# Four transposes by DMA in place of three, half-width first products, and a reordered copy at two joins

## The chip, the cores and the metric

The kernel runs on one core of a Trainium2 chip. The metric is the device time of one execution in microseconds (us), as the core's own clock has it; less is better. A profile is one execution, taken by the hardware profiler (a further one of 721.83 us for the kernel before); its span is about 1.7 us shorter than the timed figure of the same execution.

## The reference

```python
def _A_ref(x, wqkv, wo):            # 32 heads of 32, window of 8 keys, dilation 2
    q, k, v = split(x @ wqkv)
    ...                             # softmax over keys pos, pos-2, ..., pos-14
    return o @ wo

def _B_ref(x, w1, w3, w2):          # F = 3584
    return (silu(x @ w1) * (x @ w3)) @ w2

xn = layernorm(x)                   # x: 2048 tokens x 1024
s  = _A_ref(xn, wqkv, wo)
g  = silu(_B_ref(xn, w1, w3, w2))
return x + s * g
```

(Shortened: the index arithmetic of the attention is left out.)

## The kernel before

The kernel multiplies 2x2 block matrices with seven products in place of eight. Tokens lie in four blocks of 512; a pair of blocks makes the 2x2 form, and the sums and differences that the scheme needs are made on VectorE (`xs` from tokens, `sq`, `sk`, `sv` from weights). One group of products is this function. `pa`, `pe` and `pb` are PSUM buffers (two banks each, four such buffers in all); `act_copy` runs on ScalarE; `snap` is a saved copy of the first product, where it was made earlier.

```python
def seven(key, A, B, e11, e12, e22, e21, snap=None):
    a11, a12, a22, s1, s2, s3, s4 = A
    b11, b21, b22, t1, t2, t3, t4 = B
    ...                                          # pa = a11*b11, unless snap has it
    pe = bank2(f"e{key}")
    for i in I:
        mm(pe[:, i], s1[i], t1, True)            # the "inner" product
    pb = bank2(f"b{key}")
    act_copy(pb[:], pa[:] if snap is None else snap)
    sp5 = k4(f"p{key}")
    act_copy(sp5[:], pe[:])
    if snap is None:
        ...                                      # pa += a12*b21
        e11(pa)
        flush()
    for i in I:
        mm(pb[:, i], s2[i], t2, False)
    su2 = k4(f"u{key}")
    act_copy(su2[:], pb[:])
    flush()
    ...                                          # pe += s4*b22, pb += s3*t3
    def tail():                                  # the held product
        for i in I:
            mm(pb[:, i], a22[i], t4, False)
        e21(pb)
    pend.append(tail)                            # run by the next flush()
```

The normalized second block has to be transposed, tile by tile of 128 tokens. Three tiles go through the DMA queue of SyncE, one through TensorE, and its result is copied out by ScalarE:

```python
def flip(st, eng):
    cols = slice(st * P, (st + 1) * P)
    dst = b12[:, :, cols], xT[:, 2, :, cols]
    if eng == "dma":
        for a in I:
            anchor["tr1"] = nc.sync.dma_start(out=dst[a], in_=xt[1][:, st, a * CH:(a + 1) * CH], transpose=True)
        return
    tp = bank2(f"tq{st}")
    for k in range(KT):
        ...                                      # matmul(tp[...], lhsT=tile, rhs=ident)
    for a in I:
        act(nc.scalar.copy, out=dst[a], in_=tp[:, a].rearrange("p (k t) -> p k t", k=KH))
```

And these are the places where groups join:

```python
for n, cols in enumerate((slice(0, 3 * P), slice(3 * P, CH))):   # xs: three tiles, then one
    ...
qkv_seven(0, 0, wq0, wq1, sq, None, snap[0:2])
...
def tr(c):
    for sts in ([0, 1], [2, 3]):
        with behind("ln"):                       # layer norm of a later block, as early as DVE can
            ln_dve(c, sts)
...
qkv_seven(1, 1, wk0, wk1, sk, step)
flush()                                          # join 1
...
qkv_seven(0, 1, wq0, wq1, sk, step)
flush()                                          # join 2, the MLP follows
```

Of the kernel before, what the change touches and what calls it, by code (L numbers as in the profile page):

```python
# [17 lines left out]
def kernel(  # L18
# [11 lines left out]
    nc = tc.nc  # L30
    P = 128
    S, D, F = 2048, 1024, 3584
    Dh, W, DIL = 32, 8, 2
    KT = D // P
    KH = KT // 2
    CH = 512
# [9 lines left out]
    I = range(2)  # L46
# [33 lines left out]
    ident = const.tile([P, P], BF16, name="ident")  # L80
    nc.gpsimd.memset(ident[:], 0.0)
    nc.gpsimd.affine_select(
        out=ident[:], in_=ident[:], compare_op=ALU.not_equal, fill=1.0,
# [5 lines left out]
        out=ones4[:], in_=ones4[:], compare_op=ALU.is_ge, fill=0.0,  # L89
# [3 lines left out]
        out=ones4[:], in_=ones4[:], compare_op=ALU.is_ge, fill=0.0,  # L93
# [5 lines left out]
        out=maskb[0:32], in_=maskb[0:32], compare_op=ALU.is_ge, fill=-1.0e9,  # L99
# [11 lines left out]
    pb = keep.tile([P, W, P], BF16, name="pb")  # L111
    xT = keep.tile([P, 3, KH, CH], BF16, name="xT")
# [19 lines left out]
    def bank2(name):  # L132
        return psum.tile([P, 2, CH], FP32, tag="mm", name=name)

    def k4(name, shape=(2, CH), dt=FP32):
        return kk.tile([P, *shape], dt, tag="k4", name=name)
# [10 lines left out]
    def mm(ps, lhs, rhs, first):  # L147
        n = len(lhs)
        for k in range(n):
            with behind("pe") if "open" in anchor else nullcontext():  # L150
                anchor["pe"] = nc.tensor.matmul(  # L151
                    ps, lhsT=lhs[k], rhs=rhs[k], start=(first and k == 0),
                    stop=(k == n - 1), skip_group_check=not first,
                )
# [3 lines left out]

    def act_copy(out_, in_):
        with hp():  # L160
            nc.scalar.copy(out=out_, in_=in_)  # L161

    pend = []

    def flush():
        while pend:
            pend.pop(0)()

    def seven(key, A, B, e11, e12, e22, e21, snap=None):
        a11, a12, a22, s1, s2, s3, s4 = A  # L170
        b11, b21, b22, t1, t2, t3, t4 = B
        if snap is None:
            pa = bank2(f"a{key}")
            for i in I:
                mm(pa[:, i], a11[i], b11, True)
        pe = bank2(f"e{key}")
        for i in I:
            mm(pe[:, i], s1[i], t1, True)
        pb = bank2(f"b{key}")
        act_copy(pb[:], pa[:] if snap is None else snap)  # L180
        sp5 = k4(f"p{key}")
        act_copy(sp5[:], pe[:])
        if snap is None:
            for i in I:
                mm(pa[:, i], a12[i], b21, False)
            e11(pa)
            flush()
        for i in I:
            mm(pb[:, i], s2[i], t2, False)
        su2 = k4(f"u{key}")  # L190
        act_copy(su2[:], pb[:])
        flush()
        for i in I:
            mm(pe[:, i], s4[i], b22, False)
        e12(pe, su2)
        run_hooks()
        for i in I:
            mm(pb[:, i], s3[i], t3, False)
        e22(pb, sp5)
        bg(pace["n"])  # L200

        def tail():
# [4 lines that stand above are left out]
        pend.append(tail)  # L207
# [10 lines left out]
    xt = {}  # L218
    anchor = {}
# [7 lines left out]
    def behind(key):  # L227
        return tc.issue_after(anchor[key].ins) if key in anchor else nullcontext()

    def act(f, **kw):  # L230
        with hp(), behind("a"):
            anchor["a"] = f(**kw)
# [99 lines left out]
    def qkv_A(w0, w1_, st, g):  # L332
        v0 = w0.rearrange("p k (c two j) -> p k two j c", two=2, j=4)
        v1 = w1_.rearrange("p k (c two j) -> p k two j c", two=2, j=4)
        v3 = w0.bitcast(FP16).rearrange("p k (c two j) -> p k two j c", two=2, j=4)
        sv = [s.rearrange("p k (c j) -> p k j c", j=4) for s in st or ()]
        pick = lambda v, h: [[v[:, k, h, 2 * g + i, :] for k in range(KH)] for i in I]
        sp = lambda q: [[sv[q][:, k, 2 * g + i, :] for k in range(KH)] for i in I]
        if st is None:
            return pick(v0, 0), pick(v1, 0)  # L340
        return pick(v0, 0), pick(v1, 0), pick(v1, 1), sp(0), sp(1), pick(v3, 1), sp(2)
# [17 lines left out]
    def qkv_copy(t, c, j0):  # L359
        def f(ps, *a):  # L360
            d, fin = qkv_dst(t, c, j0)
            with hp():
                if a:
                    anchor["u"] = anchor.get("v")
                    anchor["v"] = nc.vector.tensor_add(d, ps[:], a[0][:])
                else:
                    nc.scalar.copy(out=d, in_=ps[:])
                fin()
        return f

    def qkv_seven(t, b, w0, w1_, st, mid=None, snaps=None):
        c0, c1 = 2 * b, 2 * b + 1
        for g in range(2):
            cp = lambda c, j0: qkv_copy(t, c, j0)
            seven(f"q{t}{b}{g}", qkv_A(w0, w1_, st, g), Bq[b],
                  cp(c0, 2 * g), cp(c1, 2 * g), cp(c1, 4 + 2 * g), cp(c0, 4 + 2 * g),
                  None if snaps is None else snaps[g])
            if mid is not None:
                mid(g)
# [122 lines left out]
    def run_hooks():  # L502
        while hooks:
            hooks.pop(0)()
# [472 lines left out]
    wq0 = qkv_load(0, 0, slot(2, (4, D)), 4)  # L977
    wq1 = qkv_load(0, 1, slot(6, (4, D)), 4)
# [9 lines left out]
    snap = [oT[:, i // 2, 4 * (i % 2):4 * (i % 2) + 4].rearrange("p j n -> p (j n)").bitcast(FP32).rearrange("p (i n) -> p i n", i=2) for i in range(4)]  # L988
# [26 lines left out]
    def root(st):  # L1015
        act(nc.scalar.activation, out=rstd[:, st:st + 1], in_=mv[:, st, 1:2], func=ACTF.Sqrt, bias=eps_t[:], scale=1.0)

    def apply(st, c=0):
        r = rstd[:, st:st + 1]
        dve(nc.vector.reciprocal, out=r, in_=r)  # L1020
        dve(
            nc.vector.tensor_scalar, out=xt[c][:, st, :], in0=xt[c][:, st, :], scalar1=mv[:, st, 0:1], scalar2=r,
            op0=ALU.subtract, op1=ALU.mult,
        )
# [60 lines left out]
    sq = rows(20, 6, FP16).rearrange("p (q k n) -> p q k n", q=3, k=4)  # L1085
    sq = [sq[:, q] for q in range(3)]
# [18 lines left out]
    b12 = rows(12, 2).rearrange("p (k n) -> p k n", k=KH)  # L1105
# [18 lines left out]
        st_half(st, 1, 1)  # L1124
        st_end(st)

    def flip(st, eng):
        cols = slice(st * P, (st + 1) * P)
        dst = b12[:, :, cols], xT[:, 2, :, cols]
        if eng == "dma":  # L1130
            for a in I:
                anchor["tr1"] = nc.sync.dma_start(out=dst[a], in_=xt[1][:, st, a * CH:(a + 1) * CH], transpose=True)
            return
        tp = bank2(f"tq{st}")
        for k in range(KT):
            with behind("pe"):
                anchor["pe"] = nc.tensor.matmul(
                    tp[:, k // KH, (k % KH) * P:(k % KH + 1) * P], lhsT=xt[1][:, st, k * P:(k + 1) * P], rhs=ident[:],
                    start=(k % KH == 0), stop=(k % KH == KH - 1), skip_group_check=True,
                )  # L1140
        for a in I:
            act(nc.scalar.copy, out=dst[a], in_=tp[:, a].rearrange("p (k t) -> p k t", k=KH))

    pf[0, 0], pf[0, 1] = pf[0], pf[1]
    s_q[1]()
# [6 lines left out]
    mean_var(1)  # L1152
    root(1)
    apply(0, 1)
    flip(0, "dma")
    first(1, 1)
    mean_var(2)
    apply(1, 1)
    flip(1, "dma")
    root(2)  # L1160
    second(1, 0)
    store(1, 0)
    second(1, 1)
    mean_var(3)
    apply(2, 1)
    root(3)
    store(1, 1)
    s_q[3]()
    apply(3, 1)
    flip(3, "dma")  # L1170
    first(2, 0)
    flip(2, "pe")
    first(2, 1)
    for g in range(2):
        second(2, g)
# [4 lines left out]

    Bq = B0, B_of(xT1[0], xT1[1], xT1[3], xs1)
    s_k = qkv_sums(wk0, wk1, sk, parts=True)
    for n, cols in enumerate((slice(0, 3 * P), slice(3 * P, CH))):
        s_k[n]()
        dve(nc.vector.tensor_sub, xs[:, 0, :, cols], b12[:, :, cols], xT[:, 0, :, cols])
        dve(nc.vector.tensor_sub, xs[:, 1, :, cols], xT[:, 2, :, cols], xs[:, 0, :, cols])
# [3 lines left out]
    with behind("ln"):  # L1190
        s_k[2]()
        s_k[3]()
    qkv_seven(0, 0, wq0, wq1, sq, None, snap[0:2])
    with behind("tr1"):
        x_load(3)
    def tr(c):
        for sts in ([0, 1], [2, 3]):
            with behind("ln"):
                ln_dve(c, sts)
        ln_tr(c, rows(*((16, 4), (12, 4))[c - 2]).rearrange("p (k n) -> p k n", k=KT))  # L1200

# [20 lines left out]
    qkv_seven(2, 0, *wv, sv, step0, snap[4:6])  # L1222
    pace["n"] = PACE[1]
    qkv_seven(1, 1, wk0, wk1, sk, step)
    flush()
    with behind("v"):
        qkv_sums(wq0, wq1, sk, True)
    qkv_seven(2, 1, *wv, sv, step)
    qkv_seven(0, 1, wq0, wq1, sk, step)
    flush()  # L1230
    spill = [(x_dram[:, i], xT1[(0, 1, 3)[i]]) for i in range(3)] + [(xs_dram[:, i], xs1[:, i]) for i in range(4)]

    def mid(b):
        drain(2 * b + 1)
        wo_prepare(b)
# [41 lines left out]
```

## Time and profile before

| | before |
|---|---|
| time, three executions | 721.73 us (721.68 to 721.85) |
| span of the profile | 720.1 us |
| TensorE busy | 712.5 us, 99% |
| VectorE busy | 625.6 us, 87% |
| ScalarE busy | 314.1 us, 44% |
| waits of TensorE after 15 us | five steps, 1.11 us in all |

In timeline lines the columns are start, length, engine, line of the kernel, operation, output and inputs, shape and count; square brackets tell how long the engine had been idle and what released it. TensorE (PE) streams its matmuls, so a gap shows as a step between starts that is longer than the columns need (0.2158 us for 512), not as a hole between an end and a start. The prediction below shows the page, the waits and the timelines of the parts concerned.

### The profile page before, as it was taken

What the parts mean: (1) busy time and instruction counts of PE and PEld (TensorE: products, weight loads), DVE (VectorE), ACT (ScalarE), POOL (GpSimd) and SP (SyncE); (2) the same over time, 40 slices, a digit from 0 to 9 for tenths busy, and PEclk for the clock granted to TensorE, in tenths of its full rate; (3) what the DMA queues carried; (4) which work ended last, traced back from release to release, by engine and by line L of the source; (5) the groups of instructions that cost most, each with busy time, mean ns of one, the idle gap of its engine ahead of it and who ended that gap; (6) DMA issues with size and microseconds to landing.
All of it is one profiled execution on the core that took longest, in us unless ns stands there. A gap on an engine that the chain in (4) does not pass through costs nothing.

```text
span 720.1 us, 8820 instructions
## 1 busy us (share of the span) xinstructions
PE 712.5 (99%) x3367; PEld 346.2 (48%) x3367; DVE 625.6 (87%) x697; ACT 314.1 (44%) x329; POOL 95.7 (13%) x162
## 2 busy tenths in 40 slices
PE   8999999999999999999999999999999999999997
PEld 6655565654444444444444444444444444444443
DVE  7996879779879878978999999969859989998975
ACT  5745334356545456555545311024464563120234
POOL 1011100012300000233111000000435004000001
PEclk9999999999999999999999999999999999999999
DMA  9956257867754523457756647469799444463616
GB/s 333 267 146 176 82 185 228 274 228 242 240 174 160 178 85 117 153 205 264 251 169 216 203 132 240 155 189 385 172 279 348 127 152 138 156 205 130 194 55 117
DMA packets 119242, 139.52 MB, mean 194 GB/s; under 512 B 17696, under 2 KB 94496, under 8 KB 118560
## 3 DMA queue, kind: packets, MB, share of 16 engines
q1 hardware_dynamic: 104656, 97.01, 43.3%
q0 software_dynamic: 14544, 41.95, 17.9%
q8 instruction: 26, 0.43, 0.3%
q14 instruction: 16, 0.13, 0.1%
HBM read 96.21 MB, written 38.80 MB: 187 GB/s over the span
## 4 chain that ended last, share of the span: by engine, by line
PE 93%; DVE 2%; ACT 1%; DMA 1%; issue 1%; SPq 0%; DVEq 0%; ACTq 0%
PE bm L151 20%; PE am L151 13%; PE em L151 13%; PE bq L151 9%; PE db L151 8%; PE da L151 7%; PE de L151 6%; PE eq L151 6%; PE aq L151 3%; PE wb L151 3%; PE af L151 2%; PE wa L151 1%; PE we L151 1%; PE af L1038 1%; DMA wring<-in_A_wqkv_dram 1%
## 5 line engine op out<-in xcount | busy, mean ns | idle before, releaser
L151 PEld LDWEIGHTS <-wring 128*128 128x128 f16 (+1 forms) x1792 | 183.4, 103 | 204.2 <-issue 1.6
L151 PEld LDWEIGHTS <-h_sb 128*128 128x128 f16 (+1 forms) x1056 | 109.6, 104 | 118.1 <-issue 0.4
L151 PE MATMUL bm<-xs,wring 128*128 128x512 f16 x504 | 117.4, 379 | 0.1
L151 PE MATMUL am<-xT,wring 128*128 128x512 bf16 x336 | 79.7, 379 | 0.1
L151 PE MATMUL db<-wring,h_sb 128*128 128x512 f16 x336 | 73.2, 379 | 0.0
L481 DVE TENSOR_TENSOR BC<-Ep,vT 128x2048 bf16<-128x2048 bf16 x56 | 66.6, 1216 | 0.1
L426 DVE TENSOR_TENSOR pt<-qt,kT 128x4096 bf16<-128x4096 bf16 x24 | 54.9, 2289 | 0.6
L664 DVE TENSOR_TENSOR um<-em,um 128x1024 f32<-128x1024 f32 x28 | 34.2, 1222 | 21.1 <-PE em L151 20.3
L666 ACT ACTIVATE g<-um 128x1024 bf16<-128x1024 f32 x28 | 29.6, 1057 | 48.6 <-DVE um L664 48.6
L151 PE MATMUL da<-wring,h_sb 128*128 128x512 bf16 x224 | 49.0, 379 | 0.0
L467 POOL DMA_DIRECT2D Ep<-pb x64 | 38.0, 601 | 54.0 <-DVE pb L463 48.3
L151 PE MATMUL bm<-h_sb,wring 128*128 128x512 f16 x168 | 39.7, 379 | 0.0
L151 PE MATMUL em<-xT,wring 128*128 128x512 bf16 x168 | 39.7, 379 | 0.0
L151 PE MATMUL em<-xs,wring 128*128 128x512 f16 x168 | 39.7, 379 | 0.0
L161 ACT COPY bm<-am 128x1024 f32<-128x1024 f32 x28 | 27.9, 998 | 26.0 <-PE am L151 26.0
L491 DVE TENSOR_TENSOR oT<-oT,BC 128x2048 bf16<-128x2048 bf16 x32 | 39.0, 1218 | 0.3
L161 ACT COPY pm<-em 128x1024 f32<-128x1024 f32 x28 | 28.4, 1013 | 20.0 <-PE em L151 20.0
L161 ACT COPY um<-bm 128x1024 f32<-128x1024 f32 x28 | 28.4, 1013 | 18.9 <-PE bm L151 18.9
L685 ACT CAST g<-bm 128x1024 bf16<-128x1024 f32 x28 | 28.3, 1010 | 17.4 <-PE bm L151 17.4
L679 DVE TENSOR_TENSOR h_sb<-bm,pm 128x1024 bf16<-128x1024 f32 x21 | 25.6, 1217 | 5.1 <-PE bm L151 5.0
L428 DVE TENSOR_TENSOR pt<-pt 128x2048 bf16<-128x2048 bf16 x24 | 29.3, 1221 | 0.4
L489 DVE TENSOR_TENSOR BC<-BC 128x2048 bf16<-128x2048 bf16 x24 | 29.3, 1220 | 0.4
(191 smaller groups left out, 996.4 us busy)
## 6 DMA issues: line engine op xcount, KB each, us to landing
wring<-in_B_w_dram SPq DMA_DIRECT2D x61, 512.0 KB, 4.4
wring<-t_dram SPq DMA_DIRECT2D x16, 512.0 KB, 3.9
t_dram<-wring POOLq DMA_DIRECT2D x14, 512.0 KB, 3.9
wring<-t_dram SPq DMA_DIRECT2D x16, 384.0 KB, 5.0
wring<-in_B_w_dram SPq DMA_DIRECT2D x12, 384.0 KB, 4.8
wring<-in_A_x_dram SPq DMA_DIRECT2D x16, 256.0 KB, 4.7
Ep<-pb POOLq DMA_DIRECT2D x64, 64.0 KB, 4.7
wring<-in_A_wo_dram SPq DMA_DIRECT2D x8, 512.0 KB, 5.7
```

The costliest lines, as they stand in the source:

```text
L151: anchor["pe"] = nc.tensor.matmul(ps, lhsT=lhs[k], rhs=rhs[k], start=(first and k == 0), stop=(k == n - 1), skip_group_check=not first,)
L161: nc.scalar.copy(out=out_, in_=in_)
L426: nc.vector.tensor_mul(p_t[:], q[:], kT[:, :, o:o + CH])
L428: nc.vector.tensor_add(p_t[:, 0:4, :], p_t[:, 0:4, :], p_t[:, 4:8, :])
L467: nc.gpsimd.dma_start(out=pr[c][r:P:NR, :, sq * P:(sq + 1) * P], in_=pb[sq * 32:(sq + 1) * 32, :, :])
L481: nc.vector.tensor_mul(dst, E[:, w, :].unsqueeze(1).to_broadcast([P, n, CH]), vT[:, js, o:o + CH])
L489: nc.vector.tensor_add(B, B, C)
L491: nc.vector.tensor_add(A, A, B if w0 else C)
L664: v = nc.vector.tensor_add(su2[:], pe[:], su2[:])
L666: nc.scalar.activation(out=hl["g"][:, :, CH:], in_=su2[:], func=ACTF.Silu)
L679: anchor["v"] = nc.vector.tensor_add(h[:, :, CH:], pb[:], sp5[:])
L685: nc.scalar.copy(out=hl["g"][:, :, 0:CH], in_=pb[:])
```

## The change

The intent is to take work and gaps out of TensorE's stream. All four tiles of the second block are transposed by DMA. Since the last tile then lands later, the sums `xs` are made in two halves of two tiles, and the first q products run in token halves: first the half that is there. The inner product of the next group (`eq1`) follows at once, so that ScalarE has time to copy out the first. At the two joins the held product isn't forced to the front any more, and its copy is told to go behind the copy that TensorE waits for. The layer norm of later blocks goes behind the adds of the first group.

```diff
     def act_copy(out_, in_):
         with hp():
-            nc.scalar.copy(out=out_, in_=in_)
+            return nc.scalar.copy(out=out_, in_=in_)
 ...
-        pe = bank2(f"e{key}")
-        for i in I:
-            mm(pe[:, i], s1[i], t1, True)
+        pe = early.pop(key)() if key in early else bank2(f"e{key}")
         pb = bank2(f"b{key}")
-        act_copy(pb[:], pa[:] if snap is None else snap)
         sp5 = k4(f"p{key}")
-        act_copy(sp5[:], pe[:])
+        if key == "q000":
+            act_copy(pb[:], snap)
+            for th in I:
+                cols = slice(th * 2 * P, (th + 1) * 2 * P)
+                for ps, A1, B1 in ((pe, s1, t1), (pb, s2, t2)):
+                    ...                      # matmuls of 256 columns
+            act_copy(sp5[:], pe[:])
+            early["q001"]()
+        else:
+            ...
+            anchor["pb"] = act_copy(pb[:], pa[:] if snap is None else snap)
+            act_copy(sp5[:], pe[:])
 ...
                 else:
-                    nc.scalar.copy(out=d, in_=ps[:])
+                    with behind("pb"):
+                        nc.scalar.copy(out=d, in_=ps[:])
 ...
-    def flip(st, eng):
+    def flip(st):
+        for a, d in enumerate((b12[:, :, cols], xT[:, 2, :, cols])):
+            anchor["tr1"] = nc.sync.dma_start(out=d, in_=xt[1][:, st, a * CH:(a + 1) * CH], transpose=True)
 ...
-    for n, cols in enumerate((slice(0, 3 * P), slice(3 * P, CH))):
+    for n, cols in enumerate((slice(0, 2 * P), slice(2 * P, CH))):
 ...
-    qkv_seven(0, 0, wq0, wq1, sq, None, snap[0:2])
+    early["q001"] = eq1                      # q001's s1*t1, 16 matmuls as before
+    qkv_seven(0, 0, wq0, wq1, sq, lambda g: anchor.setdefault("q0", anchor["v"]), snap[0:2])
 ...
-            with behind("ln"):
+            with behind("q0"):
                 ln_dve(c, sts)
 ...
     qkv_seven(1, 1, wk0, wk1, sk, step)
-    flush()
 ...
     qkv_seven(0, 1, wq0, wq1, sk, step)
-    flush()
```

More of the change, by code (lines that the diff above doesn't have):

```diff
@@ L167, in flush @@
             pend.pop(0)()
+    early = {}
     def seven(key, A, B, e11, e12, e22, e21, snap=None):
@@ L175, in seven @@
                 mm(pa[:, i], a11[i], b11, True)
-        pe = bank2(f"e{key}")
-        for i in I:
-            mm(pe[:, i], s1[i], t1, True)
+        pe = early.pop(key)() if key in early else bank2(f"e{key}")
         pb = bank2(f"b{key}")
-        act_copy(pb[:], pa[:] if snap is None else snap)
         sp5 = k4(f"p{key}")
-        act_copy(sp5[:], pe[:])
+        if key == "q000":
[3 more added lines that the diff above has]
+                for ps, A1, B1 in ((pe, s1, t1), (pb, s2, t2)):
+                    for i in I:
+                        for k in range(KH):
+                            with behind("pe"):
+                                anchor["pe"] = nc.tensor.matmul(
+                                    ps[:, i, cols], lhsT=A1[i][k], rhs=B1[k][:, cols], stop=(k == KH - 1),
+                                    start=(ps is pe and k == 0 and th == 0), skip_group_check=True,
+                                )
+            act_copy(sp5[:], pe[:])
+            early["q001"]()
+        else:
+            if key != "q001":
+                for i in I:
+                    mm(pe[:, i], s1[i], t1, True)
+            anchor["pb"] = act_copy(pb[:], pa[:] if snap is None else snap)
+            act_copy(sp5[:], pe[:])
         if snap is None:
@@ L187, in seven @@
             flush()
-        for i in I:
-            mm(pb[:, i], s2[i], t2, False)
+        if key != "q000":
+            for i in I:
+                mm(pb[:, i], s2[i], t2, False)
         su2 = k4(f"u{key}")
@@ L1125, in mean_var @@
         st_end(st)
-    def flip(st, eng):
+    def flip(st):
         cols = slice(st * P, (st + 1) * P)
-        dst = b12[:, :, cols], xT[:, 2, :, cols]
-        if eng == "dma":
-            for a in I:
-                anchor["tr1"] = nc.sync.dma_start(out=dst[a], in_=xt[1][:, st, a * CH:(a + 1) * CH], transpose=True)
-            return
-        tp = bank2(f"tq{st}")
-        for k in range(KT):
-            with behind("pe"):
-                anchor["pe"] = nc.tensor.matmul(
-                    tp[:, k // KH, (k % KH) * P:(k % KH + 1) * P], lhsT=xt[1][:, st, k * P:(k + 1) * P], rhs=ident[:],
-                    start=(k % KH == 0), stop=(k % KH == KH - 1), skip_group_check=True,
-                )
-        for a in I:
-            act(nc.scalar.copy, out=dst[a], in_=tp[:, a].rearrange("p (k t) -> p k t", k=KH))
+        for a, d in enumerate((b12[:, :, cols], xT[:, 2, :, cols])):
+            anchor["tr1"] = nc.sync.dma_start(out=d, in_=xt[1][:, st, a * CH:(a + 1) * CH], transpose=True)
     pf[0, 0], pf[0, 1] = pf[0], pf[1]
@@ L1154 @@
     apply(0, 1)
-    flip(0, "dma")
+    flip(0)
     first(1, 1)
@@ L1158 @@
     apply(1, 1)
-    flip(1, "dma")
+    flip(1)
     root(2)
@@ L1165 @@
     apply(2, 1)
+    flip(2)
     root(3)
@@ L1169 @@
     apply(3, 1)
-    flip(3, "dma")
+    flip(3)
     first(2, 0)
-    flip(2, "pe")
     first(2, 1)
@@ L1192, with eq1 @@
         s_k[3]()
-    qkv_seven(0, 0, wq0, wq1, sq, None, snap[0:2])
+    def eq1():
+        pe = bank2("eq001")
+        for i in I:
+            for k in range(KH):
+                with behind("pe"):
+                    anchor["pe"] = nc.tensor.matmul(
+                        pe[:, i], lhsT=qkv_A(wq0, wq1, sq, 1)[3][i][k], rhs=Bq[0][3][k], start=(k == 0), stop=(k == KH - 1),
+                    )
+        early["q001"] = lambda: pe
+    early["q001"] = eq1
+    qkv_seven(0, 0, wq0, wq1, sq, lambda g: anchor.setdefault("q0", anchor["v"]), snap[0:2])
     with behind("tr1"):
```

## The prediction

> **What bounds the kernel now.** I read the page first: busy shares and the slices of the span.
>
> ```profile
> span 720.1 us, 8820 instructions
> PE 712.5 (99%) x3367; PEld 346.2 (48%) x3367; DVE 625.6 (87%) x697; ACT 314.1 (44%) x329; POOL 95.7 (13%) x162
> ...
> PE   8999999999999999999999999999999999999997
> ...
> PEclk9999999999999999999999999999999999999999
> ```
>
> TensorE (PE) is busy from the second slice to the last at full granted clock. A busy PE is not yet a gapless one, so next came the waits of PE alone:
>
> ```profile
> engine line waited for: us in total, times, longest us
> PE warm L142 <- DVE warm L139: 1.3, 1, 1.3
> PE tp L993 <- DVE wring L236: 1.0, 1, 1.0
> PE af L1038 <- ACT xT L1000: 0.5, 1, 0.5
> ```
>
> These are the only waits listed for PE, and all end before 9 us. Third, PE's timeline, which begins each group where the last one stops streaming: eight 128x512 matmuls start 1.73 us apart all through the kernel, 0.2158 us each. I took the step from each matmul's start to the next and subtracted the time its columns need. After 12 us only five steps stand out: 0.28 us at 110.7, 0.24 at 160.0, 0.28 at 286.9, 0.22 at 504.6 and 0.09 at 714.4; the five-row block sums (`zp`) aside, everything else is back to back. So the time is the sum of PE's instructions plus about 1.1 us. Whatever the change does counts only where it shortens that stream, closes one of those gaps or opens a new one.
>
> The parts concerned, from PE's timeline (start, length, operation, count):
>
> ```profile
> 24.13 1.89 PE L151 MATMUL af<-xT,wve 128*128 128x512 bf16 x8
> 25.86 0.61 PE L1137 MATMUL tq<-ident,wring 128*128 128x128 bf16 x8
> 26.30 5.35 PE L151 MATMUL af<-xT,wve 128*128 128x512 bf16 x24
> 31.49 1.89 PE L151 MATMUL eq<-xs,h_sb 128*128 128x512 f16 x8
> ...
> 107.25 1.89 PE L151 MATMUL bq<-h_sb 128*128 128x512 f16 x8
> 108.97 0.38 PE L151 MATMUL aq<-h_sb,wve 128*128 128x512 bf16 x1
> 109.19 1.89 PE L151 MATMUL eq<-h_sb,wring 128*128 128x512 f16 x8
> 111.20 1.89 PE L151 MATMUL aq<-h_sb,wve 128*128 128x512 bf16 x8
> ```
>
> Three things are to be seen. The transposes of one tile by matmul take the stream from 25.86 to 26.30. The q products (`eq`) follow at once at 31.49. And `aq` at 111.20 comes 2.01 us after `eq`, not 1.73: that is the join between two products. The chain of waits says why:
>
> ```profile
> 107.41 1.74 PE bq L151 x8
> 109.15 0.03 ACTq L367
> 109.18 0.04 issue
> 109.22 1.01 ACT pk L367
> 110.23 0.92 ACT bq L161
> 111.15 0.04 issue
> 111.20 1.89 PE aq L151 x8
> ```
>
> At the join the held product (`bq`, the tail of the group before) runs first; ScalarE (ACT) copies it out (`pk`) before it makes the copy of `aq` into `bq` that lets PE overwrite `aq`. PE waits for the second copy. The join at 160 is the same: `h_sb<-bq` at 158.50, `bm<-am` from 159.41 to 160.43, PE at 160.48.
>
> **What the Trainium skill says.** "TensorE: Matmul & The Clock Gate", Back-to-back issue gap, gives N/2.4 + 2.5 ns for warm matmuls: 55.8, 109.2 and 215.8 ns for 128, 256 and 512 columns. The trace agrees: 0.44/8 = 55 ns for `tq`, 4.37/40 = 109 ns for the 128x256 products at 12.85 to 17.22, 1.73/8 = 216 ns. (The 131 ns sustained of the same section is not what this kernel shows.) "VectorE: DVE Perf Modes", The three transpose paths, gives a DMA transpose of 128x128 as 1309 ns; here one issue, of four such blocks, holds the queue for 1.19 to 1.32 us, so the figure fits an issue, not a block. "DMA: Bandwidth & Descriptors", Rules for kernel authors, advises to issue a DMA early and wait late; whether this one is early enough is the question below.
>
> **The change part by part.** The built order of instructions of the changed kernel differs only before about 162 us; from there on PE, ACT and DVE hold the same order.
>
> 1. The fourth tile of the second block is transposed by DMA too. PE loses 8 matmuls: -0.44 us. ACT loses two copies (0.58 and 0.60 us), which are off the path. The DMA queue gains two issues. This is the queue's timeline before:
>
> ```profile
> 23.58 1.21 SPq L1132 DMA_TRANSPOSE h_sb<-wring  x1
> 24.84 1.26 SPq L1132 DMA_TRANSPOSE xT<-wring  x1
> 26.70 1.19 SPq L1132 DMA_TRANSPOSE h_sb<-wring  x1
> 27.93 1.27 SPq L1132 DMA_TRANSPOSE xT<-wring  x1
> ```
>
> Tile 2 is normalized by 24.9, so its issues follow at 26.15 and 27.40, and tile 3's at about 28.7 and 29.95, ending near 31.2 instead of 29.20. The last two of before landed 1.1 us after their issues ended (29.03 and 30.31). So tile 3 lands at about 31.1 and 32.35, 2 us later than before.
>
> 2. The sums `xs` on VectorE (DVE) are split 2+2 tiles instead of 3+1, and the first q products run in token halves: `eq` half, `bq` half, `eq` half, `bq` half, then the next group's inner product. From these DVE lines
>
> ```profile
> 27.90 0.96 DVE L236 TENSOR_TENSOR xs<-h_sb,xT 128x1536 f16<-128x1536 bf16 x1
> ...
> 29.82 1.22 DVE L236 TENSOR_TENSOR h_sb<-h_sb,wring 128x2048 f16<-128x2048 f16 x1
> 30.95 0.42 DVE L236 TENSOR_TENSOR xs<-h_sb,xT 128x512 f16<-128x512 bf16 x1
> ```
>
> a 1024-wide sum is about 0.69 us. First halves: 27.9 to 28.6 and 28.7 to 29.4; `h_sb` to 30.5; then DVE waits for the landing at 31.1: second halves 31.2 to 31.9, and 32.45 to 33.15. PE reaches the q products at 31.49 - 0.45 = 31.04 and needs the four quarters at 31.04, 31.91, 32.77 and 33.64 (0.864 us each). Margins: 2.4, 2.5, 0.9 and 0.5 us. So no wait, but the last is thin. The halves cost 32 x 109.2 - 16 x 215.8 ns = +0.04 us. The next group's inner product (1.73 us) gives ACT time: `eq` is complete at 33.6, copied by 34.8, and overwritten from 36.2; `bq` at 34.5, copied by 36.8, overwritten from 37.95.
>
> 3. The layer norm of blocks 3 and 4 on DVE is put behind the first group's adds. I walked DVE's new order with the old durations: it ends near 66.9 instead of 65.7, with the last normalized tile at 63.4 instead of 56.8. Its transposes land before 70. Their sums start at 74.3, and PE reads the result at 81 to 83. No cost.
>
> 4. At the two joins the held product no longer comes first. `aq` or `am` is complete 1.73 us earlier against the copy that PE waits for, and ACT is told to make that copy first: -0.28 and -0.24 us. At the second join the order is `am` x8, held product x3, `em` x8, `am` x8, held product x5. `em` needs a weight sum of DVE, before at 156.73 to 157.41 while `em` started at 158.51. Now the sum ends at 157.41 - 0.73 = 156.68 and `em` could start at 156.70. With the weight load (103 ns) and the semaphore I allow +0.13 us.
>
> Sum: -0.44 - 0.28 - 0.24 + 0.04 + 0.13 = -0.79 us. 721.73 - 0.79 = 720.9 us.
>
> **The rivals.** (a) The DMA transposes land late, and PE waits where it had the matmul transposes. For: the queue is 2 us later, and the first two issues of before took 5.8 and 5.0 us to land, behind weight loads that ended at 26.1. Against: after 26.1 nothing else is in the queue, and the two last took 2.3 and 2.4. Each tenth beyond 0.5 us of delay is a tenth lost; 1 us more would leave 721.4. (b) The gaps at the joins only move: at the second join `em` waits for DVE, or the held product's late copy holds a PSUM buffer. For: DVE runs without idle from 155 to past 170. Against: `em` has needed this sum all along and misses it by little. If the whole of 0.24 comes back as this wait: 721.0; with a second one behind it: 721.3. (c) DVE, 87% busy, turns the delayed layer norm into waits: one of a few us would give 723 to 725. Against: it idles 5.7 us before 71.5. (d) All margins hold and `em` does not wait: 720.75.
>
> **Range and chances.** The change can take away at most about 1 us of PE's stream, and I see no stall over 1 us that it could open. I put 720.3 to 721.8 for 8 in 10: the low end is everything closed plus spread (runs of before lie 0.17 us apart), the high end a gain eaten whole by (a) or (b). Two per cent is 14 us: faster by that is impossible by the sum (0.5%), slower would need rival (c) several times over (1%), within 2% 98.5%.
>
> **What would show it.** PE's page row with 3375 matmuls (8 fewer, 16 more). `eq` near 31.05, four groups of eight 128x256 spaced 0.87, and no wait of PE there (wrong: a wait on DVE `xs` or a longer step). Transposes 7 and 8 landing near 31.1 and 32.4. `aq` at the first join 1.73 after `eq`. A step of 0.1 to 0.2 too long before `em` near 156.7. From 170 us on every PE group about 0.8 us earlier than before, with the gaps at 287 and 504 unchanged. The prediction is wrong if any stage after 170 us changes its own length.

## The result, and the profile after

The kernel after took 721.28 us (median of six, 721.25 to 721.94), the kernel before in the same session 721.91 us (six, 721.68 to 722.16). The ratio is 0.9993, with a 95% interval of 0.998 to 1.0006: the same, at 2%. A ratio is the mean time of one kernel's fast runs over that of the other's of the same rounds, so it isn't quite the ratio of the medians.

The page of the kernel after, and the waits of TensorE behind the one at its start (1.3 us, as before), with total, count and longest in us:

```profile
span 719.6 us, 8835 instructions
PE 712.4 (99%) x3375; PEld 347.6 (48%) x3375; DVE 625.5 (87%) x697; ACT 313.1 (44%) x327; POOL 95.7 (13%) x162
```

```profile
PE tp L1013 <- DVE wring L255: 0.5, 2, 0.3
PE af L1058 <- ACT xT L1020: 0.4, 1, 0.4
```

TensorE has 3375 matmuls (8 fewer and 16 more), ScalarE two copies fewer, and no new wait of TensorE is listed. The front in TensorE's timeline after:

```profile
24.09 7.07 PE L151 MATMUL af<-xT,wve 128*128 128x512 bf16 x32
31.00 1.04 PE L189 MATMUL eq<-xs,h_sb 128*128 128x256 f16 x8
31.87 1.04 PE L189 MATMUL bq<-xs,h_sb 128*128 128x256 f16 x8
32.74 1.04 PE L189 MATMUL eq<-xs,h_sb 128*128 128x256 f16 x8
33.62 1.04 PE L189 MATMUL bq<-xs,h_sb 128*128 128x256 f16 x8
34.49 1.89 PE L1207 MATMUL eq<-xs,h_sb 128*128 128x512 f16 x8
36.22 1.89 PE L151 MATMUL eq<-xT,h_sb 128*128 128x512 bf16 x8
```

The transposes by matmul are gone from the stream, the q products begin at 31.00 and not at 31.49, and the four half-width groups follow each other at 0.87 us. The two sums that had to wait for the last tile are these in VectorE's timeline:

```profile
30.64 0.69 DVE L255 TENSOR_TENSOR xs<-h_sb,xT 128x1024 f16<-128x1024 bf16 x1 [0.87 <-DMA h_sb<-wring]
31.95 0.69 DVE L255 TENSOR_TENSOR xs<-xT,xs 128x1024 f16<-128x1024 bf16 x1 [0.61 <-DMA xT<-wring]
```

VectorE waits for each landing (30.54 and 31.82), but its results, at 31.33 and 32.64, are 1.41 and 0.98 us ahead of the third and fourth group of TensorE.

The first join, with ScalarE's copies, after:

```profile
107.01 1.89 PE L151 MATMUL eq<-h_sb,wring 128*128 128x512 f16 x8
107.21 1.00 ACT L161 COPY bq<-aq 128x1024 f32<-128x1024 f32 x1 [4.12 <-PE aq L151]
108.73 1.89 PE L151 MATMUL aq<-h_sb,wve 128*128 128x512 bf16 x8
...
110.46 1.89 PE L151 MATMUL bq<-h_sb 128*128 128x512 f16 x8
110.66 1.01 ACT L387 CAST pk<-aq 128x1024 bf16<-128x1024 f32 x1 [0.67 <-PE aq L151]
```

The copy of `aq` (107.21) now starts 3.4 us ahead of the next `pk`, and `aq` at 108.73 follows `eq` after 1.72 us: the gap is closed. The second join in TensorE's timeline, after:

```profile
156.05 0.81 PE L151 MATMUL bq<-h_sb,wring 128*128 128x512 f16 x3
156.75 1.90 PE L151 MATMUL em<-xs,wring 128*128 128x512 f16 x8
158.48 1.89 PE L151 MATMUL am<-xT,wring 128*128 128x512 bf16 x8
160.21 1.03 PE L151 MATMUL bq<-h_sb,wring 128*128 128x512 f16 x4
```

Three matmuls take 0.65 us, so `em` could have started at 156.70; it lost 0.05 us, and `am` lost nothing.

From there on, nothing in TensorE's order differs. So the same group late in the kernel tells the total; from the chains of waits of before and of after:

```profile
549.20 3.45 PE bm L151 x16
...
700.07 2.59 PE wa L151 x12
```

```profile
548.29 3.45 PE bm L151 x16
...
699.16 2.59 PE wa L151 x12
```

Both are 0.91 us earlier, and so is VectorE's last add:

```profile
717.04 0.42 DVE L969 TENSOR_TENSOR h_sb<-h_sb,xw 128x512 bf16<-128x512 bf16 x1
```

```profile
716.13 0.43 DVE L989 TENSOR_TENSOR h_sb<-h_sb,xw 128x512 bf16<-128x512 bf16 x1
```

The last output transfer lands at 719.17 before and 718.26 after, again 0.91 us earlier. Yet the span is only 0.53 us shorter (720.13 and 719.60). The rest, 0.38 us, is given back after the last landing, in 0.96 us before and 1.34 us after. There the kernels do nothing but end. These are the instructions of the closing line in either kernel, before first:

```profile
L1272 SPq EVENT_SEMAPHORE  x11: 17/28/28, 717.9 to 720.1; - x11
L1272 SPq DRAIN  x3: 7/7/7, 719.3 to 719.6; - x3
```

```profile
L1290 SPq EVENT_SEMAPHORE  x11: 17/28/28, 717.0 to 719.5; - x11
L1290 SPq DRAIN  x3: 7/7/7, 718.8 to 719.1; - x3
```

The columns are duration in ns (least, median, most), then the first and last start. Before, SyncE's first drain starts 0.14 us after the landing at 719.17; after, 0.51 us after the one at 718.26. I read the single events of SyncE from the trace; start in us, and the number of the DMA semaphore awaited:

```
before                              after
717.494 issue of last output, 109   716.587 issue of last output, 101
717.936 wait 101                    718.272 wait 101   <- released by the last landing
717.998 wait 104                    718.334 wait 104
718.062 wait 105                    718.398 wait 105
718.124 wait 106                    718.460 wait 106
718.183 wait 107                    718.519 wait 107
718.554 wait 108                    718.581 wait 108
719.184 wait 109  <- last landing   718.640 wait 109
719.245 wait 110                    718.702 wait 110
719.310 drain                       718.767 drain
```

SyncE waits for its queue's eight semaphores in this fixed order in both kernels, 0.062 us for each that is already through. (Each of these instructions awaits a second semaphore too; those of other DMA queues had their last landing before 712 us.) Its transfers take the eight in rotation, without an exception in any of the ten traces. The kernel before has 239 of them, so the last takes the seventh semaphore, and one wait comes behind it. The two additional transposes make it 241: the last takes the first semaphore, and seven waits come behind it. Six waits of 0.062 us are 0.37 us.

The ledger, against the kernel before:

| place | predicted, us | in the trace, us |
|---|---|---|
| start of the stream at 24 us (early loads, differs from run to run) | 0 | -0.04 |
| eight transposing matmuls gone | -0.44 | -0.45 |
| products in halves | +0.04 | +0.04 |
| first join | -0.28 | -0.28 |
| `em` waits for VectorE | +0.13 | +0.05 |
| second join | -0.24 | -0.23 |
| after the last landing | 0 | +0.38 |
| sum | -0.79 | -0.53 |

(The trace's sum is within 0.01 us of the span's difference.)

### The profile page after: what moved, and what is told of

The parts are those of the page before. It is cut to its first block, busy times and chain, and to the rows that moved or that the text cites. A ratio compares the mean times of both kernels' runs of the same rounds, so it can differ in the third digit from the quotient of the medians.

```text
span 719.6 us, 8835 instructions
## 1 busy us (share of the span) xinstructions
PE 712.4 (99%) x3375; PEld 347.6 (48%) x3375; DVE 625.5 (87%) x697; ACT 313.1 (44%) x327; POOL 95.7 (13%) x162
## 4 chain that ended last, share of the span: by engine, by line
PE 96%; DVE 1%; ACT 1%; DMA 0%; issue 0%
PE bm L151 20%; PE am L151 13%; PE em L151 13%; PE db L151 10%; PE bq L151 8%; PE de L151 7%; PE da L151 7%; PE eq L151 5%; PE aq L151 3%; PE wb L151 3%; PE af L151 2%; PE we L151 2%; PE wa L151 2%; DVE h_sb L255 1%; PE af L1058 1%; DMA wring<-in_A_x_dram 0%
## 5 line engine op out<-in xcount | busy, mean ns | idle before, releaser
L151 PEld LDWEIGHTS <-h_sb 128*128 128x128 f16 (+1 forms) x1032 | 106.9, 104 | 115.6 <-issue 0.4
```

The costliest lines, as they stand in the source:

```text
L151: anchor["pe"] = nc.tensor.matmul(ps, lhsT=lhs[k], rhs=rhs[k], start=(first and k == 0), stop=(k == n - 1), skip_group_check=not first,)
```

## The experiments

My theory: the parts of the change do what the ledger says, and 0.38 us is lost because the last output changed its place among SyncE's closing waits, which only the number of transfers decides. The rival for the end: the end differs by chance, or because of the new instructions themselves, and the number of transfers has nothing to do with it. The rivals for the front: half-width products, the early inner product and the later layer norm are decoration, and the gain would be there without them.

The first four ran on one chip; the kernel before took 721.74 us there (nine executions, 721.62 to 721.95). The last four ran on another; there it took 721.80 us (nine, 721.57 to 722.11). Every kernel's results were correct. "Last matmul" is the start of TensorE's last matmul in the profile (before 715.37, after 714.45), "end" the time from the last landing to the end of the span.

| run | time, us: median (all) | ratio (95%) | last matmul | end |
|---|---|---|---|---|
| after_again | 721.35 (721.24 to 722.18) | 0.9996 (0.9984 to 1.0009) | 714.52 | 1.33 |
| one_dma_fewer | 720.98 (720.82 to 721.95) | 0.9992 (0.9979 to 1.0004) | 714.64 | 0.90 |
| before_two_more | 722.00 (721.94 to 722.28) | 1.0005 (0.9992 to 1.0017) | 715.32 | 1.33 |
| joins_only | 721.47 (721.41 to 721.94) | 0.9999 (0.9985 to 1.0012) | 714.93 | 0.97 |
| front_only | 721.86 (721.78 to 721.94) | 1.0001 (0.9987 to 1.0014) | 715.02 | 1.34 |
| whole_products | 723.98 (722.84 to 724.29) | 1.0027 (1.0015 to 1.004) | 717.45 | 1.33 |
| halves_no_early | 721.65 (721.47 to 722.21) | 0.9999 (0.9987 to 1.0012) | 715.38 | 1.33 |
| ln_in_old_place | 728.40 (727.83 to 728.76) | 1.0091 (1.0077 to 1.0104) | 721.68 | 1.33 |

All runs have five executions, ln_in_old_place four. At 2% each of them is the same as the kernel before. The intervals are about 0.13% to either side, 0.9 us. Only whole_products and ln_in_old_place are separated from 1 by them; the rest is told apart by the traces, and the medians go along.

### The kernel after once more

No edit; it is the yardstick for the runs beside it.

> The changed kernel itself, as the base for the others on this chip. Its matmuls should again end some 0.9 us earlier than those of the kernel before, and its time be 0.5 to 0.65 us shorter (721.3 us where the kernel before has 721.9). If the difference between the two gains (0.38 us) was chance of one profiled run, this profile will show another stretch between the last landing and the end than 1.34 us; if it is built in, it will show 1.34 again.

It came to 721.35 us, 0.39 below the kernel before on this chip, with the same 1.33 us at the end.

### One transfer fewer

```diff
-        for st in range(NST):
+        for st in range(NST - 2 * (c == 3)):
             ...
+        if c == 3:                    # tiles 2 and 3 of the last block in one transfer
+            g = c * NST + 2
+            nc.sync.dma_start(out=xt[c][:, 2:4, :], in_=x_flat[g * P:(g + 2) * P, :].rearrange("(s p) d -> p s d", p=P))
```

> The changed kernel with two loads of block 4 joined into one, so that every later transfer of the SyncE queue takes the semaphore before, and the last output transfer takes the last one that is waited for at the end instead of the first. Theory (the waits at the end stand in a fixed order, 0.062 us each, and those behind the last landing cost time): seven waits fewer behind the last landing, so the end comes 0.90 us after it instead of 1.34, and the time is 0.43 us under that of the changed kernel: about 720.85 us. Rival (the end takes as long as it takes; the two profiles differ by chance): the time of the changed kernel, 721.3 us. All matmuls stand in the same order in both.

With 240 transfers the last output takes the eighth semaphore, and nothing is left to wait for behind it. SyncE's drains in the closing line of this run:

```profile
L1293 SPq DRAIN  x3: 7/7/7, 718.5 to 718.8; - x3
```

The last landing is at 718.45 and the first drain at 718.53. The end took 0.90 us, 0.43 less than in the run beside it, which is seven waits of 0.062 us. The median fell by 0.37 us, although the early loads of this profile came 0.12 us later (the weights' first product at 24.28, beside 24.16), which put everything behind them later. This is the best version that I have: 0.76 us under the kernel before by the medians.

### Two transfers more in the kernel before

```diff
         for st in range(NST):
             g = c * NST + st
-            nc.sync.dma_start(out=xt[c][:, st, :], in_=x_flat[g * P:(g + 1) * P, :])
+            for h in range(2 if c == 3 and st > 1 else 1):    # two loads cut in halves
+                d = slice(h * CH, (h + 1) * CH) if c == 3 and st > 1 else slice(0, D)
+                nc.sync.dma_start(out=xt[c][:, st, d], in_=x_flat[g * P:(g + 1) * P, d])
```

> The kernel before with two loads of block 4 each cut in two halves: two transfers more, as in the changed kernel, and nothing else changed. Theory: the last output transfer moves from the seventh semaphore waited for to the first, six waits of 0.062 us come behind it, and the time rises by 0.38 us over the kernel before (722.3 where that has 721.9) with PE's matmuls ending at the same time. Rival: no difference.

Nothing of the change is in this kernel, only its number of transfers. The last landing is at 719.11, the end took 1.33 us as in the kernel after, and the drain lies half a microsecond behind the landing, in the same row of this run:

```profile
L1274 SPq DRAIN  x3: 7/7/7, 719.6 to 719.9; - x3
```

The median rose by 0.26 us, a little less than the 0.37 of the trace; in the profile the stream began 0.05 us earlier. With this run, the one before it and the joins alone (239 transfers, 0.97 us at the end) the rival for the end falls: the end follows the number of transfers in both kernels, in both directions, by the step that the trace shows. It rests on the traces: by the timed intervals alone none of these runs is apart from the kernel before.

### The joins alone

```diff
# in the kernel before: only these parts of the change
+            return nc.scalar.copy(out=out_, in_=in_)            # act_copy
+        anchor["pb"] = act_copy(pb[:], pa[:] if snap is None else snap)
+                    with behind("pb"):
                         nc.scalar.copy(out=d, in_=ps[:])
-    flush()                                                     # both joins
```

> The kernel before with the two joins changed alone. Theory: PE closes 0.28 and 0.24 us and loses 0.05 before em, so its matmuls end 0.47 us earlier; the count of transfers is that of before, so the end keeps its 0.96 us after the last landing: time 0.47 us shorter (721.45 where the kernel before has 721.9). Rival: the closed gaps come back later as waits on DVE or on a PSUM buffer, and the time is that of before.

TensorE's last matmul starts 0.44 us earlier than before; the end stays 0.97. In the timeline of this run the first join reads as in the kernel after, the copy first:

```profile
107.68 1.00 ACT L161 COPY bq<-aq 128x1024 f32<-128x1024 f32 x1 [4.12 <-PE aq L151]
109.21 1.89 PE L151 MATMUL aq<-h_sb,wve 128*128 128x512 bf16 x8
```

The median is 0.27 us lower and not 0.44; the profiled execution, 721.41 us, is 0.33 lower than before's median. The trace's figure is within the scatter of that. No run separates the two parts of this change, the flushes left out and the copy told to go behind.

### The front alone

```diff
# in the kernel after: the joins put back
-                    with behind("pb"):
-                        nc.scalar.copy(out=d, in_=ps[:])
+                    nc.scalar.copy(out=d, in_=ps[:])
+    flush()                                                     # at both joins
```

> The changed kernel with the two joins put back as they were: the fourth tile by DMA, token halves and the early inner product alone. Theory: PE's matmuls end 0.4 to 0.45 us earlier than in the kernel before (eight transposes gone), but the two transfers more put six waits behind the last landing (0.38 us): the time is 0.0 to 0.1 us shorter, thus the same as before within the spread. Rival: this part is worth its 0.44 us in the time as well, and something else costs the changed kernel its 0.38 us.

The stream ends 0.35 us earlier than before (the early loads came 0.06 us later in this profile; -0.45 + 0.04 + 0.06 = -0.35), the end 0.38 us longer, and the time is the same within 0.06 us of the medians. The join's gap is back, from the chain of waits of this run:

```profile
108.87 1.01 ACT pk L386
109.88 0.92 ACT bq L161
110.80 0.04 issue
110.85 1.24 PE aq L151 x5
```

So the whole front, transposes and halves together, was worth nothing in time as it was built: its two additional transfers cost at the end what they saved at the start.

### Whole products

```diff
-        if key == "q000":
+        if key == "none":             # q products whole, none in halves
 ...
-    early["q001"] = eq1
```

> The changed kernel with the first q products whole again, in the old order (all tiles by DMA, sums split 2+2). Theory: the first product now needs the sum over all four tiles at 31.0 us, which DVE finishes at about 31.35 (it waits for the landing at 30.5); PE waits 0.35 us, or up to 0.95 if the front runs as late as it did in the profile of before; so 0.3 to 0.9 us over the changed kernel, and most of the gain of the removed transposes is gone. Rival (the halves are not needed, the DMA is early enough): within 0.05 us of the changed kernel or even 0.04 less.

```profile
31.47 0.69 DVE L253 TENSOR_TENSOR xs<-h_sb,xT 128x1024 f16<-128x1024 bf16 x1 [0.95 <-DMA h_sb<-wring]
32.22 1.92 PE L151 MATMUL eq<-xs,h_sb 128*128 128x512 f16 x8 [0.80 <-DVE xs L253]
```

The wait is where it was expected: the landing releases VectorE, VectorE's sum releases TensorE, and the step is 0.96 us too long. With halves, the same sum has until the third group. I had expected 0.3 to 0.9 us on the time, and it was over 2, because a second stall of 1.65 us came at 142.8. (In this profile, the slowest of the five executions, the stream also began 0.26 us later and lost 0.14 us at 58.3.) The chain of waits there:

```profile
126.08 5.40 DMA t_dram<-wring
...
132.01 9.64 DMA v_dram<-pk
...
141.75 1.02 ACT uq L161
...
142.81 1.89 PE bq L151 x8
```

A store of v keeps a buffer that ScalarE's copy `uq` needs, and this time it landed only after 9.64 us. In the kernel after, the store in its place was issued at 129.24 and landed at 134.50. The next run shows what went before it.

### Halves, but no early inner product

```diff
             act_copy(sp5[:], pe[:])
-            early["q001"]()
         else:
-            if key != "q001":
-                for i in I:
-                    mm(pe[:, i], s1[i], t1, True)
+            for i in I:
+                mm(pe[:, i], s1[i], t1, True)
 ...
-    early["q001"] = eq1
```

> The changed kernel with the token halves, but the next group's inner product back in its old place. Theory: ACT cannot copy eq and bq between the last half and the products that overwrite them: eq is copied by 34.85 us while PE would come to it at 34.7, and bq by 36.7 while PE would come at 36.6, so PE waits 0.2 to 0.4 us in all and the time rises by as much over the changed kernel. Rival: ACT is quick enough, no difference.

The steps before the two groups after the halves are 0.18 us (at 34.80) and 0.14 us (at 36.66) too long, 0.32 together, as expected: ScalarE's copies of `eq` and `bq` end at 34.75 and 36.61, and TensorE overwrites each 0.05 us later. In the kernel after the same two copies end at 34.84 and 36.69, 1.4 and 1.25 us before TensorE comes to it (36.22 and 37.94), since the early product lies between. The profiled execution was also the slowest of the five, 722.21 us, and it shows the stall of the run above in small, 0.70 us; from its chain of waits:

```profile
124.96 4.97 DMA t_dram<-wring
129.93 0.02 SPq L729
...
130.46 9.12 DMA v_dram<-pk
...
139.68 1.02 ACT uq L161
```

In SyncE's order a weight load stands ahead of the store and waits for a store of `t_dram` that landed at 129.93, so the store of v is issued at 130.46, just behind a large fetch of q (130.14). In the kernel after it was issued at 129.24, ahead of that fetch (129.92). All ten profiles agree: in eight the store is issued 0.68 us ahead of the fetch and lands 4.8 to 5.8 us later; in this run and in the whole products it is issued behind the fetch and lands after 9.1 and 9.6 us, and only these two have the stall. So it is a race, and losing it cost 0.7 and 1.65 us; but no run set the order by itself, so that the order is the cause stays argued. The two fastest of the five executions took 721.47 us, 0.74 below the profiled one, as if without the stall. It is likely that this race is also behind the single slow executions of the kernel after (721.94 and 722.18); none of them was profiled, and the kernel before had one of 722.16 us too, so this stays open.

### The layer norm in its old place

```diff
     def tr(c):
         for sts in ([0, 1], [2, 3]):
-            with behind("q0"):
+            with behind("ln"):
                 ln_dve(c, sts)
```

> The changed kernel with the layer norm of blocks 3 and 4 tied where it was, not behind the first group's adds. In the built order DVE then does nine statistics and a normalization before the first add. Theory: the add comes at about 43 us instead of 38.2; ACT's copy of the second eq waits for it (its buffer is the add's), and PE, which reaches the product that overwrites eq at 43.1, waits about 2 us: time 722.5 to 724. Rival: the place of the layer norm does not matter, as DVE has 5 us of idle time before 71; no difference.

I had expected about 2 us and it was 7. First ScalarE's copy `pq` in the kernel after, with what released it, then the timeline of this run:

```profile
39.47 1.01 ACT L161 COPY pq<-eq 128x1024 f32<-128x1024 f32 x1 [2.78 <-DVE pk L384]
```

```profile
42.82 1.22 DVE L384 TENSOR_TENSOR pk<-eq,uq 128x1024 bf16<-128x1024 f32 x1
...
44.64 0.29 ACT L270 ACTIVATE rstd<-mv,eps_t 128x2 f32<-128x2 f32 x1 [3.73 <-DVE mv L268]
44.85 0.99 ACT L161 COPY pq<-eq 128x1024 f32<-128x1024 f32 x1
...
45.89 0.58 PE L151 MATMUL eq<-xT,h_sb 128*128 128x512 bf16 x1 [4.26 <-ACT pq L161]
46.34 3.57 PE L151 MATMUL bq<-xs,wring 128*128 128x512 f16 x8
```

ScalarE's copy `pq` waits for VectorE's first add (`pk<-eq,uq`), and TensorE waits for the copy: a step 4.43 us too long. By the times of the traces it has three parts. The add came behind eight statistics, as expected (42.82; I had said about 43), and ended at 44.04: with the kernel after's order of matmuls that is a wait of 1.9 us, the 2 us that I had expected. A square root (`rstd`) stood ahead of the copy and held it until 44.85, 0.8 us more. And the built order had moved a matmul that overwrites `eq` ahead of the eight of `bq`, so that TensorE came to it 1.73 us sooner. These parts add up to 4.43, but were not tested one by one. Then eight matmuls of 512 columns took 3.57 us, not 1.89. The stretches of five microseconds from 40, with busy time and count by engine, then granted clock, DMA share and GB/s, show why:

```profile
40.00:45.00 5.00, 1.63 (x8) 0.75 (x7) 5.00 (x12) 0.65 (x3) 0.65 (x1) 0.96 0.21 48
45.00:50.00 5.00, 4.11 (x10) 1.57 (x10) 5.00 (x12) 1.90 (x3) 0.66 (x2) 0.50 0.84 215
50.00:55.00 5.00, 5.00 (x21) 2.61 (x20) 3.04 (x6) 2.07 (x3) 0.54 (x1) 0.86 0.24 57
```

The granted clock fell to half, for 13 matmuls at 0.43 us, 2.7 us more. The Trainium skill says so, "TensorE: Matmul & The Clock Gate", Part 1: after an idle window of about 3.4 us the array goes back to half rate. The trace agrees: 4.43 us without a matmul did it (the clock fell at 44.61, 3.1 us after the last column had streamed), and the 1.65 us of the whole products did not. So moving the layer norm isn't decoration either: of the parts that I took away one at a time, it is the costliest to lose. It is needed only beside the rest of the change, though: in the kernel before, the layer norm stood in this place too, the add came behind three statistics, at 38.09, and TensorE lost nothing there.

## Why the prediction was right

The time on record was 720.9 us with a range of 720.3 to 721.8; the kernel took 721.28, and 721.35 on another occasion. It is the same within 2%, as it was given 98.5%. By its own steps:

- **The stream.** The step from counted instructions to microseconds held to 0.01 us, for the eight transposing matmuls and for the 32 half-width ones in place of 16. The reason is that TensorE had no slack anywhere near: what leaves a gapless stream comes off the end.
- **The landing.** The two additional transposes were expected at 31.1 and 32.35, and came at 30.54 and 31.82, because VectorE, and with it the issue of the transposes, ran some 0.5 us earlier in this profile. That was luck of the run: after_again has 31.14 and 32.42, as predicted, and one_dma_fewer 31.36 and 32.63, where the last sum ends 0.36 us before TensorE comes to it, with no wait either. Rival (a), a late landing, did not come true, and the whole products show what it would have cost.
- **The layer norm.** VectorE's new order was expected to end near 66.9, with the last normalized tile at 63.4; it ended at 66.4, and that tile came at 63.0. The sums that follow start at 73.82 (expected 74.3). No cost, as said, and rival (c) is out.
- **The joins.** -0.28 and -0.23 for -0.28 and -0.24; the joins alone gave them without the rest.
- **`em`.** This term was mis-sized: +0.13 expected, +0.05 measured. I had added a whole weight load (0.10) and a semaphore to the end of VectorE's sum. In the trace the sum ends at 156.69, the weight load starts at 156.74 and `em` at 156.75, beside the load and not behind it. (Without this term the prediction's own figures give 720.81 for its case (d), not 720.75.)
- **What failed.** The prediction named what would make it wrong: any stage after 170 us that changes its own length. One did, the very last. I took the time from the last landing to the end as constant, without asking what it is made of, and counted the two additional transfers only where they land. They cost 0.38 us at the end, half of the gain that I had summed. That is as much as the difference between 720.9 and the measured median, but in part by chance: in the spans the sum was missed by 0.26, since `em` and an earlier start gave 0.12 back, and the kernel before had a median of 721.91 when it ran beside the changed kernel, not the 721.73 that I had started from.

## What to carry to other kernels

When TensorE is gapless, count: matmuls times columns, plus the steps that are too long, gives a change to hundredths of a microsecond, and one late group compared between two traces checks the sum. Then look behind the last landing as well: on a kernel that ends with SyncE's waits, the number of transfers modulo eight is worth up to 0.43 us here (of the eight remainders three were run), and a transfer more or fewer anywhere, where it costs nothing, can put the last output in the best place. And when work moves on VectorE, look at what then stands ahead of the instructions that TensorE waits for: in the costliest experiment here eight statistics stood ahead of an add on VectorE, and a square root ahead of a copy on ScalarE.

## What the Trainium skill lacked or had wrong

- No page has the order or the cost of SyncE's DMA waits at the end: it waits for its eight DMA semaphores in a fixed order, 0.062 us each, so that the time from the last landing to the end was 0.90, 0.96 to 0.97 or 1.33 to 1.34 us, with 240, 239 and 241 transfers of that queue. It would belong to "DMA: Bandwidth & Descriptors".
- "TensorE: Matmul & The Clock Gate", Back-to-back issue gap, gives about 131 ns for a sustained stream at 512 columns, and says that its formula counts too much there. In this kernel, which alternates weight loads and matmuls without a gap, it is 216 ns, as the formula has it.
- "VectorE: DVE Perf Modes", The three transpose paths, gives 390 ns for a transpose of 128x128 on TensorE and 1309 ns by DMA. Inside a stream of matmuls the former took 55 ns here, and one DMA issue of four such blocks held the queue for 1.21 to 1.33 us; in the kernel after the last four landed 2.3 to 2.5 us after they began, the first four 3.5 to 5.9. By the page's numbers the choice looks like 390 against 1309; in this kernel it is 0.44 us of the bounding engine against nothing on it, as long as the landing is in time (and, by the number of transfers, 0.37 us at the end).
